# First chunk's MLP in float32 on unsplit weights, weights split later, and the scores of two units in one run, in an attention and MLP kernel

## The chip, the cores and the metric

The kernel runs on one core of one Trainium2 chip. A core has a matrix engine (TensorE, PE in the profile, with PEld for its weight loads), VectorE (DVE), ScalarE (ACT), GpSimd (POOL) and SyncE (SP, here used to issue DMAs). The metric is the device time in microseconds; less is better.

## The reference

Attention in two parts over 8 batches and 8 heads, with 512 local and 32 global rows of 64 numbers each, and then a two-layer MLP over all 8 x 544 = 4352 rows. The weights of the MLP arrive as 64-bit floats.

```python
k_all = np.concatenate([k_g, k_l], axis=2); v_all = np.concatenate([v_g, v_l], axis=2)
out_g = np.matmul(sm(scale * np.matmul(q_g, k_all.transpose(0, 1, 3, 2))), v_all)
mask = np.abs(pos[:, None] - pos[None, :]) <= 32
s_ll = np.where(mask, scale * np.matmul(q_l, k_l.transpose(0, 1, 3, 2)), -1000000000.0)
s_lg = scale * np.matmul(q_l, k_g.transpose(0, 1, 3, 2))
out_l = np.matmul(sm(np.concatenate([s_lg, s_ll], axis=-1)), np.concatenate([v_g, v_l], axis=2))
x = np.concatenate([out_g, out_l], axis=2)      # then as (4352, 512), heads side by side
h = x @ w_in                                    # 512 -> 2048
g = 0.5 * h * (1.0 + erf(h / sqrt(2)))
return g @ w_out                                # 2048 -> 512
```

## The kernel before

**Tiling.** The local rows are worked in 16 chunks of 256 rows (a batch and a half of it, `key = (b, half)`), the global rows of all batches as a seventeenth chunk `"g"`. A chunk's attention has four units `(b, half, p)`, one for each pair of heads, and gives the chunk's input x, transposed, in `xs` (512 x 256). The chunk's MLP then goes over 16 column blocks f of 128: first-layer products (`h`, four row blocks c of x, L727 to L729), gelu on ACT for two blocks at a time (`gf`), and second-layer products into two accumulators (`acc`, L758 to L760).

**Split products.** Except in the first eight units, every product is made in float32r with its operands split into a rounded part and the rest, as three passes (high x high, high x low, low x high). So each MLP product has three matmul passes, and x, the gelu output and the weights are each split by a copy (`xh`, `gh`, first half of `wi` and `wo`) and a subtraction (`xl`, `gl`, second half). The first eight units (`NF32`) multiply unsplit float32 instead.

**Weights.** Each of 32 weight tiles n (even: a block of `w_in`, odd: of `w_out`; 512 KB as 64-bit numbers) is loaded into one of seven buffers (`w_load`), turned into float32 bits in three steps (`w_1`, `w_2` on ACT, `w_3` on DVE), and split (`w_4` copies, `w_5` subtracts) into `wi` and `wo`. The first chunk's products wait for `w_5`.

**A unit's steps.** Keys and queries are loaded, transposed (for the first eight units on PE, L362 to L370, later on DVE), and copied or split; scores on PE (`st_s`, L440: pairs of matmuls on the two halves of the array's rows), masks and maxima on DVE (L459), exponentials on ACT, normalization on DVE, transposes on PE (L514 to L517), copies, and the output product (L563 in the first eight units, L550 later). `sg`, `gt`, `go` and `gx` are the global rows' scores, transposes and products.

**What sets the order.** Every step is a node with needs, buffers that it takes and frees, the engines it may run on, an assumed duration (`DUR`) and a due time. A planner in the kernel starts, on the engine that is free first, the ready step that is due first, and the instructions are issued in that order, which each engine then keeps. Due times come from a base per chunk (`C = 60.0` us each), and tables of offsets by kind (`OFF`, `OFF0`).

Of the kernel before, what the change touches and what calls it, by code (L numbers as in the profile page):

```python
# [84 lines left out]
def attn_mlp(ctx, tc, q_l, k_l, v_l, q_g, k_g, v_g, w_in, w_out, out):  # L100
# [31 lines left out]
    for half in range(2):  # L132
        m = cp.tile([P, WS + WF], BF16, name=f"mask{half}")
        nc.gpsimd.memset(m, 0.0)


        if half == 0:
            runs = [(0, 0, 128), (160, 128, 32),
                    (WS, -32, 32), (WS + 64, 0, 160)]
        else:  # L140
            runs = [(0, -32, 32), (64, 0, 128),
                    (WS, -32, 160), (WS + 192, 128, 32)]
        for c0, k0, w in runs:
# [10 lines left out]

    def copy(e, out, in_):
        if e == "a":
# [3 lines left out]
        else:  # L160
            nc.gpsimd.tensor_copy(out=out, in_=in_)

    def sub(e, **kw):
        (nc.vector if e == "v" else nc.gpsimd).tensor_sub(**kw)  # L164

# [951 lines left out]
```

## Time and profile before

| | us |
|---|---|
| median of 3 runs (lowest, highest) | 1057.42 (1057.25, 1058.53) |
| span of the profiled execution, first to last instruction | 1052.2 |
| PE without work, summed over the span | 31.1 |
| of it before 220 us | 26.0 |

The profile shows one execution. A row of its groups or of its timeline names the source line, the engine, the operation, output and inputs, the shape, and how many; in a group the two numbers after the bar are the time that its instructions cover in us and the mean of one in ns, and behind the second bar stands how long the engine was idle just before them. A timeline row has start and length in us ahead. Times of PE instructions overlap, since it works in a pipeline, so its pace is read from start to start. "PEclk" is the share of the full clock that was granted to PE.

### The profile page before, as it was taken

The page shows a single profiled execution, that of the slowest core. Times are in us where ns is not written, and L with a number is a line of the kernel's source. Part 1 is how long each engine was busy: PE and PEld are TensorE (multiplying, and loading weights), DVE is VectorE, ACT ScalarE, POOL GpSimd, SP SyncE. Part 2 cuts the span into 40 slices and gives each one's busy share as a digit, 9 for nine tenths or more (in the row PEclk, how much of TensorE's full clock was granted, in tenths as well). Part 3 has the DMA queues.
Part 4 walks back from the last instruction along what each step waited for, and adds up shares of the span by engine and source line. Part 5 has one row for each costly group of instructions (what it writes and reads, how often), then busy time and mean ns, then how long its engine had stood idle before and what let it go on. Part 6 is the DMA issues. An engine that isn't in the chain of part 4 may idle for free.

```text
span 1052.2 us, 21637 instructions
## 1 busy us (share of the span) xinstructions
PE 1021.1 (97%) x7096; PEld 911.2 (87%) x7096; DVE 716.5 (68%) x2168; ACT 745.3 (71%) x1650; POOL 355.2 (34%) x407
## 2 busy tenths in 40 slices
PE   4799999999999999999999999999999999999998
PEld 3488788889899889998998989998999989999896
DVE  5898866775867777777868777777868768661000
ACT  6886887677769686787769686787779686774231
POOL 3232345334333433234323433234323434243121
PEclk9899999999999999999999999999999999999999
DMA  8756333322222232223222332223231332101000
GB/s 243 205 149 197 84 84 64 78 51 68 45 59 38 60 74 49 56 52 79 44 63 38 65 71 47 55 53 78 44 66 38 64 67 50 46 14 34 1 21 21
DMA packets 273233, 71.27 MB, mean 68 GB/s; under 512 B 258528, under 2 KB 266720, under 8 KB 273120
## 3 DMA queue, kind: packets, MB, share of 16 engines
q1 hardware_dynamic: 269808, 65.03, 27.6%
q10 hardware_dynamic: 3312, 4.85, 1.5%
q8 instruction: 56, 0.92, 0.4%
q14 instruction: 57, 0.47, 0.1%
HBM read 60.88 MB, written 8.91 MB: 66 GB/s over the span
## 4 chain that ended last, share of the span: by engine, by line
PE 87%; DVE 3%; DMA 3%; ACT 3%; issue 2%; SPq 1%; POOL 1%; ACTq 0%; POOLq 0%; DVEq 0%
PE h L727 11%; PE h L729 11%; PE h L728 11%; PE acc L758 11%; PE acc L760 11%; PE acc L759 11%; PE o L550 5%; PE s L440 5%; PE t L514 3%; PE go L678 2%; PE sg L593 2%; DMA wraw<-in_moe_w_in_dram 1%; PE t L515 1%; ACT a_t L323 1%; PE o L563 1%
## 5 line engine op out<-in xcount | busy, mean ns | idle before, releaser
L164 POOL TENSOR_TENSOR gl<-gf,gh 128x512 fp32r<-128x512 f32 x135 | 176.7, 1309 | 459.6 <-DVE gh L159 247.4
L727 PE MATMUL h<-xh,wi 128*128 128x256 f32 x1088 | 315.0, 290 | 1.3 <-ACT xh L157 1.3
L728 PE MATMUL h<-xl,wi 128*128 128x256 f32 x1088 | 303.9, 279 | 0.5 <-POOL xl L164 0.4
L729 PE MATMUL h<-xh,wi 128*128 128x256 f32 x1088 | 303.6, 279 | 0.0
L758 PE MATMUL acc<-wo,gh 128*128 128x512 f32 x544 | 219.7, 404 | 0.0
L727 PEld LDWEIGHTS h<-xh,wi 128*128 128x128 f32 x1088 | 204.2, 188 | 12.5 <-ACT xh L157 1.7
L760 PE MATMUL acc<-wo,gh 128*128 128x512 f32 x544 | 214.9, 395 | 0.0
L759 PE MATMUL acc<-wo,gl 128*128 128x512 f32 x544 | 214.8, 395 | 0.0
L728 PEld LDWEIGHTS h<-xl,wi 128*128 128x128 f32 x1088 | 204.6, 188 | 6.8 <-POOL xl L164 0.6
L729 PEld LDWEIGHTS h<-xh,wi 128*128 128x128 f32 x1088 | 204.2, 188 | 0.0
L323 ACT ACT_TABLE_LOAD x129 | 165.5, 1283 | 40.3 <-PE h L729 38.6
L323 ACT ACTIVATE gf<-h 128x512 f32<-128x512 f32 x136 | 81.2, 597 | 76.2 <-PE h L729 73.4
L760 PEld LDWEIGHTS acc<-wo,gh 128*128 128x128 f32 x544 | 102.1, 188 | 24.5
L323 ACT ACTIVATE a_t<-a_t,sm 128x192 f32<-128x192 f32 (+1 forms) x256 | 117.0, 459 | 1.4 <-DVE sm L465 0.6
L759 PEld LDWEIGHTS acc<-wo,gl 128*128 128x128 f32 x544 | 102.4, 188 | 13.2 <-POOL gl L164 0.3
L758 PEld LDWEIGHTS acc<-wo,gh 128*128 128x128 f32 x544 | 102.2, 188 | 13.4
L164 POOL TENSOR_TENSOR vs<-vr,vs 128x512 fp32r<-128x512 f32 x56 | 72.6, 1297 | 120.1 <-ACT vs L157 53.1
L459 DVE CUSTOM_DVE_ANT_0 a_t<-s,mask 128x192 f32<-128x192 f32 (+1 forms) x256 | 80.8, 369 | 27.9 <-PE s L440 27.7
L534 DVE TENSOR_TENSOR at<-t,at 128x512 fp32r<-128x512 f32 x112 | 67.8, 619 | 23.3 <-ACT at L157 22.0
L550 PE MATMUL o<-at,vs 128*128 128x256 f32 x448 | 74.2, 288 | 0.2
L157 ACT ACTIVATE at<-t 128x512 fp32r<-128x512 f32 x112 | 59.1, 542 | 21.6 <-PE t L517 10.4
L550 PEld LDWEIGHTS o<-at,vs 128*128 128x128 f32 x448 | 63.0, 188 | 8.3 <-issue 2.1
(121 smaller groups left out, 1618.8 us busy)
## 6 DMA issues: line engine op xcount, KB each, us to landing
raws<-in_v_l_dram SPq DMA_DIRECT2D x64, 128.0 KB, 2.4
out_dram<-ob SPq DMA_DIRECT2D x32, 256.0 KB, 2.1
raws<-in_k_l_dram SPq DMA_DIRECT2D x224, 36.0 KB, 2.0
vr<-in_v_l_dram SPq DMA_DIRECT2D x116, 64.0 KB, 2.1
raws<-in_q_l_dram SPq DMA_DIRECT2D x224, 32.0 KB, 1.9
wraw<-in_moe_w_out_dram SPq DMA_DIRECT2D x12, 512.0 KB, 4.0
wraw<-in_moe_w_in_dram SPq DMA_DIRECT2D x11, 512.0 KB, 4.7
wraw<-in_moe_w_in_dram ACTq DMA_DIRECT2D x5, 512.0 KB, 4.3
```

What stands on the lines that cost most here:

```text
L157: nc.scalar.activation(out=out, in_=in_, func=AF.Copy)
L164: (nc.vector if e == "v" else nc.gpsimd).tensor_sub(**kw)
L323: nc.scalar.activation(func=func, **kw)
L459: nc.vector.tensor_tensor_reduce(out=a_t[:, j, aoff[half][i]:aoff[half][i] + w], in0=s[:, c:c + w], in1=masks[half][:, c:c + w], scale=1.0 ...
L534: nc.vector.tensor_sub(out=at[:, 1], in0=st.pop((u, "t", j))[:, :n * P].rearrange("p (n q) -> p n q", q=P), in1=at.bitcast(F32)[:, 0])
L550: nc.tensor.matmul(out=o[:, :, qsl], lhsT=l.rearrange("p s e -> p (s e)"), rhs=r, start=(n == 0), stop=(n == 3), skip_group_check=True)
L727: nc.tensor.matmul(out=h, lhsT=hi, rhs=xh, start=(c == 0 and not (key == (0, 0) and f < HQ and f % 2)), stop=False, skip_group_check=True)
L728: nc.tensor.matmul(out=h, lhsT=hi, rhs=xl, start=False, stop=False, skip_group_check=True)
L729: nc.tensor.matmul(out=h, lhsT=lo, rhs=xh, start=False, stop=(c == NCC - 1), skip_group_check=True)
L758: nc.tensor.matmul(out=acc[t], lhsT=gh[:, f % 2, tsl], rhs=hi, start=(f == 0), stop=False)
L759: nc.tensor.matmul(out=acc[t], lhsT=gl[:, f % 2, tsl], rhs=hi, start=False, stop=False)
L760: nc.tensor.matmul(out=acc[t], lhsT=gh[:, f % 2, tsl], rhs=lo, start=False, stop=(f == NF - 1))
```

## The change

The first chunk's MLP multiplies unsplit float32: x comes straight from the output product into `xf`, the weights from `w_3` (`wf`), the gelu output is not split, and each product is one float32 matmul (two instructions on PE) instead of three. Its steps wait for `w_3`, no longer for the split. `w_4` and `w_5` run later, after the last weight tile is loaded and converted and after chunk 0 has used the tile; chunk 1 waits for `w_5`. The loads of weights have 16 buffers, with at most six loads ahead of `w_1` (`NW`); half of the `w_1` steps may go to DVE. From the ninth unit on, the scores of two units are one step (`st_s2`), the second unit's in two banks of the pool of transposes. The first units' keys, queries and values have a second set of buffers (`rawb`, `vrb`), and some of these loads are issued by ACT. The global rows go to DRAM (`gu_w`) and are read back at the end (`ml_xg`). The masks are stored once for both halves. Due times and offsets are new.

```diff
-    "ah": 3.7, "al": 7.1, "b": -0.8, "c": -23.8, "e": -38.8, "g": -16.9, "gagh": 2.4, "gagl": -24.7,
...
+    "ah": (-1660.8, 999.4, -180.5, -284.0), "al": (-88.1, -183.9, -1009.5, -128.3), "b": (103.5, -531.0, -610.7, -1679.5),
...
+NW = 6
...
+    wp = ctx.enter_context(tc.tile_pool(name="wp", bufs=2 * NF + 1))
+    wr = ctx.enter_context(tc.tile_pool(name="wr", bufs=NF))
...
     def w_1(e, n):
...
+        raw = wraw[n]
+        if e == "v":
+            nc.vector.tensor_single_scalar(out=raw[:, 0::2], in_=raw[:, 0::2], scalar=29, op=ALU.logical_shift_right)
+        else:
+            nc.scalar.activation(out=raw[:, 0::2], in_=raw.bitcast(U16)[:, 1::4], func=AF.Copy, scale=2.0 ** -13, bias=-0.5 + 2.0 ** -14)
...
     def w_3(e, n):
...
+        raw = wraw.pop(n)
+        wf[n] = wp.tile([P, 512], F32, name="wf", tag="w")
+        nc.vector.scalar_tensor_tensor(out=wf[n].bitcast(I32), in0=raw[:, 1::2], scalar=3, in1=raw[:, 0::2],
                                        op0=ALU.logical_shift_left, op1=ALU.bitwise_or)
...
+    def w_4(e, i, n):
+        if i % 2 == 0:
+            wh["t"] = wr.tile([P, 1024], F32R, name="wh", tag="wr")
+        wh[n] = wh["t"][:, i % 2 * 512:i % 2 * 512 + 512]
+        copy(e, wh[n], wf[n])
 
     def w_5(e, n):
...
+        wl_[n] = lo = wp.tile([P, 512], F32R, name="wl", tag="w")
+        sub(e, out=lo, in0=wf.pop(n), in1=wh[n].bitcast(F32))
...
+    def st_s2(e, u, x):
+        st_s(e, u)
+        st_s(e, x, 1)
+
+    def st_s(e, u, other=0):
         half = u[1]
+        i = u[2] % 2
         for jj in range(2):
-            st[u, "s", jj] = ps_s.tile([P, 512], F32, name="s", tag="s")
+            st[u, "s", jj] = (ps_t if other else ps_s).tile([P, 512], F32, name="s", tag="t" if other else "s")
...
     def st_c0(e, u):
         o = st.pop((u, "o", 0))
+        x = xs[:, u[2]]
+        if u[:2] == (0, 0):
+            st["xf", u[2]] = x = xp.tile([P, CH], F32, name="xf", tag=f"xh{u[2]}")
         for j in range(2):
-            copy(e, xs[64 * j:64 * j + 64, u[2]], o[0:64, j])
+            copy(e, x[64 * j:64 * j + 64], o[0:64, j])
...
+    def gu_w(e, g, i):
+        b, p = g[0], 2 * g[1] + i
+        nc.sync.dma_start(out=xg[:, p, b * SG:b * SG + SG], in_=st.pop((g, i, "c")))
+
+    def ml_xg(e):
+        nc.sync.dma_start(out=xs, in_=xg)
...
         h = st["h", key, f // 2][:, f % 2]
+        if key == (0, 0):
+            nc.tensor.matmul(out=h, lhsT=wf[2 * f][:, c * P:c * P + P], rhs=st["xf", c], start=(c == 0 and not (f < HQ and f % 2)), stop=(c == NCC - 1), skip_group_check=True)
+            return
...
+        acc = st[key, "acc"]
+        if key == (0, 0):
+            for t in range(2):
+                nc.tensor.matmul(out=acc[t], lhsT=st[key, "gf", f // 2][:, f % 2, t * P:t * P + P], rhs=wf[2 * f + 1], start=(f == 0), stop=(f == NF - 1))
+            return
...
-    C = 60.0
+    CS = [28.0] + [106.0 + 60.0 * c for c in range(2 * B)]
+    CW = [4.3] + [3.75] * (2 * B)
...
+        step(("w4", n), w_4, (i, n), "va", due + 60.0, [("w3", wl[NF + i // 2]), ("wl", wl[-1])] + ([("w4", wl[i - 1])] if i else []), [("wr", ("h", n))] if i % 2 == 0 else [])
+        step(("w5", n), w_5, (n,), "pv", due + 61.0, [("w4", n), ("w5", wl[i - 1]) if i else ("w3", wl[-1])] + used)
...
+        elif odd:
+            step(("s", u), st_s2, (pu, u), "t", s0, [(x, y) for x in ("q1", "k1", "q2", "k2") for y in (pu, u)] + [("s", units[n - 2])],
+                 [(x, (y, "s", j)) for x, y in (("s", pu), ("t", u)) for j in range(2)] + [(x, y) for y in (pu, u) for x in ("sm", "a%d" % (y[2] % 2))],
...
+            w = [("w3", 2 * f)] if not n else [("w5", 2 * f)] if n == 1 else []
...
+        elif nm[0] == "wl" and wl.index(nm[1]) >= NW:
+            tc.add_manual_dep(ins[seen], w1s[wl[wl.index(nm[1]) - NW]], mybir.DependencyInfo(mybir.DependencyClass.Sync, mybir.DependencyReason.DATA), reason="throttle")
```

What moves is seen best in the order in which each engine gets its instructions. Three places follow; the line numbers are those of the respective kernel.

**PE, where the first MLP begins.** Before, from the output product (`o`) of the first chunk's fourth unit on; `s` are the next unit's scores, `qp` transposed queries:

```order
L563 MATMUL o_597<-ao_589,vr 64x128
L563 MATMUL o_597<-ao_593,vr 64x128
L563 MATMUL o_597<-ao_589,vr 64x128 x2
L440 MATMUL s<-kt,qt 128x192 x2
L440 MATMUL s<-kt,qt 128x224 x2
L370 MATMUL qp<-ident,raws 128x128 x2
L727 MATMUL h<-xh,wi 128x256
L728 MATMUL h<-xl,wi 128x256
L729 MATMUL h<-xh,wi 128x256
```

Now, from the output product of the first unit on (`t` are transposes of the second unit's weights):

```order
L530 MATMUL o_357<-ao_340,vr 64x128 x2
L563 MATMUL sg<-kt,gs 128x288
L705 MATMUL h<-xf,wf 128x256 x3
L480 MATMUL t<-ident,a_t_122 128x128 x2
L481 MATMUL t<-ident,ge 128x128
L483 MATMUL t<-ident,ge 128x128
L327 MATMUL qp<-ident,raws 128x128 x2
```

The first products of the MLP stand behind the first unit instead of the fourth. In all 12 of the 64 (each two instructions on PE) stand ahead of the fourth unit's output product, those of the first three head pairs with the first four weight blocks.

**PE, a run of scores in a later chunk.** Before, one unit (`k` and `q` are the split operands):

```order
L440 MATMUL s<-k_141,q_143 128x192 x2
L440 MATMUL s<-k_141,q_144 128x192 x2
L440 MATMUL s<-k_142,q_143 128x192 x2
L440 MATMUL s<-k_141,q_143 128x224 x2
L440 MATMUL s<-k_141,q_144 128x224 x2
L440 MATMUL s<-k_142,q_143 128x224 x2
```

Now, the same step for two units, between MLP products:

```order
L406 MATMUL s<-k_4792,q_4883 128x192 x2
L406 MATMUL s<-k_4792,q_4902 128x192 x2
L406 MATMUL s<-k_4797,q_4883 128x192 x2
L406 MATMUL s<-k_4792,q_4883 128x224 x2
L406 MATMUL s<-k_4792,q_4902 128x224 x2
L406 MATMUL s<-k_4797,q_4883 128x224 x2
L406 MATMUL s<-k_4931,q_5008 128x192 x2
L406 MATMUL s<-k_4931,q_5037 128x192 x2
L406 MATMUL s<-k_4956,q_5008 128x192 x2
L406 MATMUL s<-k_4931,q_5008 128x224 x2
L406 MATMUL s<-k_4931,q_5037 128x224 x2
L406 MATMUL s<-k_4956,q_5008 128x224 x2
```

The second unit's six rows follow the first one's without anything between. From the ninth unit on all 56 units go in 28 such runs.

**ACT, the head of its queue.** Before (`wraw` is a weight tile, `kt` the first unit's keys, copied from the transposes):

```order
L183 DMA wraw<-in_moe_w_in_dram 128x4x256 x2
L200 ACT_TABLE_LOAD
L200 ACTIVATE wraw<-wraw 128x512
L204 ACTIVATE wraw<-wraw 128x512
L157 ACTIVATE kt<-kp 128x320
```

Now (`vr` and `vrb` are values, `gs` the global queries):

```order
L262 DMA vr<-in_v_l_dram 32x2x64 x2
L312 DMA raws<-in_q_l_dram 128x4x64 x2
L374 ACT_TABLE_LOAD
L374 ACTIVATE gs<-qg 64x4x32 x2
L251 DMA vrb<-in_v_l_dram 128x4x64 x2
L259 DMA vrb<-in_v_l_dram 32x4x64
L259 DMA vrb<-in_v_g_dram 32x4x64
L259 DMA vrb<-in_v_l_dram 64x4x64
L262 DMA vrb<-in_v_g_dram 32x2x64 x2
L262 DMA vrb<-in_v_l_dram 32x2x64 x2
L132 ACTIVATE kt<-kp 128x320
L150 DMA wraw<-in_moe_w_in_dram 128x4x256
```

The loads of the first four units' values and of the first queries (20 issues in all, seven of them ahead of these rows) now stand ahead of the first copy, and the first weights behind it.

More of the change, by code (lines that the diff above doesn't have):

```diff
@@ L132, in attn_mlp @@
     for half in range(2):
-        m = cp.tile([P, WS + WF], BF16, name=f"mask{half}")
+        m = cp.tile([P, WF], BF16, name=f"mask{half}")
         nc.gpsimd.memset(m, 0.0)
[L137 to L143, printed above, removed]
+        for c0, k0, w in (((0, -32, 32), (64, 0, 160)) if half == 0 else ((0, -32, 160), (192, 128, 32))):
             v = m[:, c0:c0 + w]
@@ L242, in attn_mlp @@
     qraw = raws[:, 928:1184].rearrange("p (c e) -> p c e", e=32)
[L244 to L254 removed]
+    agt = lp.tile([P, 4, 2, 2, SG], F32R, name="agt")
+    agg = lp.tile([P, 2, 2, 2, SG], F32R, name="agg")
+    for i in range(2):
+        nc.vector.tensor_copy(out=agg[:, i], in_=zero)
     def quads():
@@ L665, in gu_vc @@
     def gu_vc(e, g, i):
-        copy(e, late["vgs"][:, :, 0, :], gvr)
+        if "vgs" not in st:
+            st["vgs"] = lp.tile([P, 10, 2, D], F32R, name="vgs", tag="vgs")
+        copy(e, st["vgs"][:, :, 0, :], gvr)
     def gu_vl(e, g, i):
-        t = late["vgs"]
+        t = st["vgs"]
         sub(e, out=t[:, :, 1, :], in0=gvr, in1=t.bitcast(F32)[:, :, 0, :])
     def gu_o(e, g, i):
-        a = [late["agt"][:, n] for n in range(4)] + [late["agg"][:, i]]
+        a = [agt[:, n] for n in range(4)] + [agg[:, i]]
         o = ps_s.tile([P, 2, 2, D], F32, name="go", tag="s")
@@ L735, in ml_g @@
     def ml_g(e, key, f):
[L736 removed]
+        gf = gp.tile([P, 2, CH], F32, name="gf", tag="gh") if key == (0, 0) else gp.tile([P, 2, CH], F32, name="gf", tag="gf", bufs=1)
         st[key, "gf", f] = gf
@@ L838, in attn_mlp @@
             if not odd:
-                step(("lk", u), load_kn, (u,), "s", s0 - 15.0, [], [("kn", u)], issues=5 + half, size=0.33, after=("lk", units[n - 2]) if n else None)
-                step(("lq", u), load_qn, (u,), "s", s0 - 14.0, [], [("qn", u)], issues=2, size=0.26, after=("lq", units[n - 2]) if n else None)
-            step(("tk", u), st_tkn, (u,), "t", s0 - 5.0, [("lk", pair)] + pv(("tq",)), [("h", (u, "k"))], [("kn", pair), ("kgr", b)], dur="tkn")
-            step(("tq", u), st_tqn, (u,), "t", s0 - 3.5, [("lq", pair)], [("h", (u, "q"))], [("qn", pair)], dur="tqn")
+                step(("lk", u), load_kn, (u,), "s", s0 - 15.0, [], [("kn%d" % second(u), u)], issues=5 + half, size=0.33, after=("lk", units[n - 2]) if n else None)
@@ L843, in attn_mlp @@
+                step(("lq", u), load_qn, (u,), "sa" if n < 4 else "s", s0 - 14.0, [], [("qn%d" % second(u), u)], issues=2, size=0.26, after=("lq", units[n - 2]) if n else None)
+            step(("tk", u), st_tkn, (u,), "t", s0 - 5.0, [("lk", pair)] + pv(("tq",)), [("h", (u, "k"))], [("kn%d" % second(u), pair), ("kgr", b)], dur="tkn")
+            step(("tq", u), st_tqn, (u,), "t", s0 - 3.5, [("lq", pair)], [("h", (u, "q"))], [("qn%d" % second(u), pair)], dur="tqn")
             kb, qb = [("h", (u, "k"))], [("h", (u, "q"))]
@@ L880, in attn_mlp @@
         if n < NPE and not odd:
-            step(("lv", u), load_v, (u, 2), "s", f0 - 18.0, [], [("vr0", u), ("vr1", units[n + 1])], issues=9, size=0.5, after=("lv", units[n - 2]) if n else None)
+            step(("lv", u), load_v, (u, 2), "sa" if n < 4 else "s", f0 - 18.0, [], [("vs", (u, "r"))] if second(u) else [("vr0", u), ("vr1", units[n + 1])], issues=9, size=0.5, after=("lv", units[n - 2]) if n else None)
             step(("vm", u), st_vm, (u, 2), "p", f0 - 8.0, [("lv", u)])
@@ L953, in attn_mlp @@
         for f in range(NF // 2):
             d = C0 + W * (2 * f + 2)
-            step(("g", key, f), ml_g, (key, f), "a", d, [("hc", key, x, NCC - 1) for x in (2 * f, 2 * f + 1)] if not n and 2 * f < HQ else [("h", key, 2 * f + 1) if 2 * f + 1 < NF - 1 else ("hc", key, NF - 1, NCC - 1)], [("gf", (key, f))], [("h", (key, f)) if n or 2 * f >= HQ else ("acc", "h")], table="gelu")
-            step(("gh", key, f), ml_gh, (key, f), "av", d + 0.7, [("g", key, f)], [("gh", (key, f))], early=not n)
@@ L957, in attn_mlp @@
-            step(("gl", key, f), ml_gl, (key, f), "v" if key == "g" and f == NF // 2 - 1 else "p", d + 1.3, [("gh", key, f)], [("gl", (key, f))], [("gf", (key, f))], early=not n)
+            step(("g", key, f), ml_g, (key, f), "a", d, [("hc", key, x, NCC - 1) for x in (2 * f, 2 * f + 1)] if not n and 2 * f < HQ else [("h", key, 2 * f + 1) if 2 * f + 1 < NF - 1 else ("hc", key, NF - 1, NCC - 1)], [("gf" if n else "gh", (key, f))], [("h", (key, f)) if n or 2 * f >= HQ else ("acc", "h")], table="gelu")
```

347 lines of the change are left out of this document (168 added, 179 removed), and 25 rows, old and new, of tables (DUR, OFF, OFF0).

## The prediction

> **What bounds the kernel now.** I read the page's busy times first, then sums by stage, because a mean over the whole span hides that the stages have different limits.
>
> ```profile
> PE 1021.1 (97%) x7096; PEld 911.2 (87%) x7096; DVE 716.5 (68%) x2168; ACT 745.3 (71%) x1650; POOL 355.2 (34%) x407
> ```
>
> The sums by stage (first the stretch in us and its length, then each engine's busy time and instructions):
>
> ```profile
> core 0: us, PE busy (x) PEld busy (x) DVE busy (x) ACT busy (x) POOL busy (x), PEclk, DMA share, GB/s
> 0.00:15.20 15.20, 4.89 (x18) 2.65 (x18) 4.63 (x10) 6.28 (x11) 7.72 (x28) 1.00 0.76 210
> 15.20:56.50 41.30, 31.04 (x166) 22.48 (x167) 36.61 (x107) 36.79 (x94) 9.03 (x10) 0.88 0.74 215
> 56.50:116.50 60.00, 56.73 (x376) 49.27 (x377) 50.75 (x122) 44.43 (x93) 15.74 (x18) 0.97 0.62 165
> 116.50:220.00 103.50, 101.33 (x719) 90.33 (x719) 77.74 (x242) 80.44 (x186) 45.30 (x50) 1.00 0.34 74
> 220.00:940.00 720.00, 719.91 (x5145) 650.90 (x5145) 536.00 (x1660) 543.29 (x1201) 249.65 (x279) 1.00 0.26 55
> 940.00:1052.20 112.20, 107.21 (x680) 95.59 (x678) 10.76 (x28) 34.11 (x69) 27.72 (x22) 1.00 0.06 19
> ```
>
> From 220 to 940 us TensorE (PE) is busy for 719.91 of 720 us at full clock: there only fewer or shorter PE instructions save time, and what DVE, ACT or POOL do counts only if PE comes to wait for it. The last stage has 5.0 us without PE work (its final copies and stores), which the change leaves as it is. All other idle PE time lies before 220 us: 10.3 us up to 15.2, 10.3 up to 56.5 (at a clock of 0.88), then 3.3 and 2.2. The first MLP matmul starts right at 56.5:
>
> ```profile
> 56.58 0.36 PE L727 MATMUL h<-xh,wi 128*128 128x256 f32 x1
> ```
>
> Between 15.2 and 56.5 DVE and ACT are each busy 89% of the time: they bound that stage, not PE (75%). So four terms make the sum: when the first chunk's attention is done (A), what its MLP then costs PE (B), what the joined score runs save (C), and what PE waits after that (D). All are differences against this profiled execution, whose span is 1052.2 us; the median of the runs, 1057.4, is 5.2 us more (launch and end, which the change doesn't touch), so I take the differences from the median.
>
> **A: when chunk 0's attention is done.** What DVE does in that stage:
>
> ```profile
> L208 DVE SCALAR_TENSOR_TENSOR wraw<-wraw 128x512 int32<-128x512 int32 x13 | 8.8, 687 | 0.0
> L459 DVE CUSTOM_DVE_ANT_0 a_t<-s,mask 128x224 f32<-128x224 f32 x10 | 3.8, 384 | 0.0
> L493 DVE TENSOR_TENSOR a_t<-a_t,sm 128x512 f32<-128x512 f32 x4 | 3.6, 902 | 0.1
> L459 DVE CUSTOM_DVE_ANT_0 a_t<-s,mask 128x192 f32<-128x192 f32 x10 | 3.5, 350 | 1.0 <-PE s L440 1.0
> L164 DVE TENSOR_TENSOR wo<-wraw,wo 128x512 fp32r<-128x512 f32 x4 | 2.8, 698 | 0.0
> L164 DVE TENSOR_TENSOR wi<-wraw,wi 128x512 fp32r<-128x512 f32 x4 | 2.8, 693 | 0.1
> L159 DVE CAST xh<-xs 128x256 fp32r<-128x256 f32 x3 | 1.8, 653 | 0.0
> L159 DVE CAST wi<-wraw 128x512 fp32r<-128x512 f32 x4 | 1.7, 424 | 0.1
> L159 DVE CAST wo<-wraw 128x512 fp32r<-128x512 f32 x2 | 0.8, 418 | 0.0
> L500 DVE TENSOR_TENSOR ge<-a_t,sm 128x256 f32<-128x256 f32 x2 | 0.8, 418 | 0.0
> ```
>
> In the new order DVE has, from the first mask-and-maximum step up to the copy of unit 3's output (the last input of the first MLP), no weight splits and no xh or xl: minus 8 x 0.70 (the second halves, wi and wo), 6 x 0.42 (the first halves), about 2.2 for xh and xl, and one conversion of 12 instead of 13 (0.7), also two small products that POOL takes (0.6): 11.6 us less. It has more: five first conversion steps that were ACT's (no row shows them on DVE; between 0.42, the plain copy of this size, and 0.74; I take 0.69, the step on the same tile: 3.4), a sixth unit's four mask steps (1.5) and a fifth normalization (1.3), three more 128x256 products (1.3), and small copies (0.9): 8.4. Net 3.2 us less. With the same 4.7 us of idle time DVE comes to that copy at 15.2 + 36.6 - 3.2 + 4.7 = 53.3 instead of 56.5. **A = -3.2.** With no idle time it would be 48.6 (-7.9); if the weights come late it is no earlier than now (+1). ACT's own work in that stage falls from 36.8 to about 33 by the same count, so DVE stays the later one.
>
> Nothing is won at the very start. ACT's queue now issues 20 loads ahead of its first copy, and SP eight small ones ahead of the first keys:
>
> ```profile
> 6.03 2.38 SPq L282 DMA_DIRECT2D qgr<-in_q_g_dram  x4
> 8.45 0.98 SPq L296 DMA_DIRECT2D vr<-in_v_l_dram  x2
> 13.26 1.86 PE L440 MATMUL s<-kt,qt 64*128 64x192 f32 x8
> ```
>
> At 0.5 us per issue (0.98 for two) ACT is through at about 0.7 + 10 + 1.3 for its table + 0.6, nearly 13 us; SP's keys are issued by 0.7 + 8 x 0.6 + 5 x 0.55 = 8.3. The first scores thus start behind ACT's copy, near 13.5, as now (13.26). The first weights, which head ACT's queue now, are issued at 13 to 18 us; twelve of them (6.3 MB) and 1.5 MB of attention input need 36 us at the stage's 215 GB/s, till about 50. That is just ahead of DVE, so a start no earlier than now stays in the range.
>
> **B: the first MLP in float32.** One of its products is two passes, each at half the rate, instead of three passes at the full one.
>
> ```profile
> 24.84 1.96 PE L563 MATMUL o<-ao,vr 128*64 128x128 f32 x16
> ...
> L563 PE MATMUL o<-ao,vr x16: 272/272/323, 24.8 to 26.5; 128*64 128x128 f32 x16
> ...
> 58.67 0.70 PE L593 MATMUL sg<-kt,gs 128*128 128x256 f32 x2
> ...
> 299.83 0.28 PE L728 MATMUL h<-xl,wi 128*128 128x256 f32 x1
> 299.95 0.28 PE L729 MATMUL h<-xh,wi 128*128 128x256 f32 x1
> 300.07 0.40 PE L758 MATMUL acc<-wo,gh 128*128 128x512 f32 x1
> 300.30 0.40 PE L759 MATMUL acc<-wo,gl 128*128 128x512 f32 x1
> ```
>
> (The second row gives one instruction's shortest, median and longest time in ns; "f32" stands for split operands too.) Split passes start 0.12 us apart at 256 columns and 0.23 at 512. A chunk has 192 + 96 of them: 23.0 + 22.1 = 45.1 us. A float32 pass over 128 columns takes 0.11 us: sixteen in 1.96, of which the last one's tail is 0.27, so 1.69/15; that makes 0.22 and 0.44; the two passes of 256 columns at 58.67 agree (0.70 less a start-up of 0.1 and an end of 0.16 leaves 0.22 each). 128 x 0.22 + 64 x 0.44 = 56.3, thus 11.2 us more (10.7 with 0.109 per pass, 12.5 with 0.113). But twelve of the 64 first-layer products stand in the new order ahead of unit 3's output product, where PE is idle a quarter of the time: 12 x 0.44 = 5.3 us are hidden. **B = +5.9.** Without that cover it is +11.2.
>
> The Trainium skill ("TensorE: Matmul & The Clock Gate", Weight-path perf modes — Fast Weight Load (FWL) and DoubleRow) speaks against this part: fast weight load is on for 128 weights unless the type is FP32, so a float32 product would load its stationary half more slowly. The trace's shortest float32 load is as short as a split one, in the rows under the rivals.
>
> **C: scores of two units in one run.**
>
> ```profile
> 308.56 0.28 PE L729 MATMUL h<-xh,wi 128*128 128x256 f32 x1
> 308.77 0.93 PE L440 MATMUL s<-k,q 64*128 64x192 f32 x12
> 309.63 0.39 PE L727 MATMUL h<-xh,wi 128*128 128x256 f32 x1
> 309.85 0.28 PE L728 MATMUL h<-xl,wi 128*128 128x256 f32 x1
> ...
> 309.19 0.51 PE L440 MATMUL s<-k,q 64*128 64x224 f32 x6
> ...
> L440 PE MATMUL s<-k,q x24: 268/272/355, 210.3 to 220.6; 64*128 64x192 f32 x12, 64*128 64x224 f32 x12
> ```
>
> From the last h pass to the second one behind the run are 1.29 us; without the run it would be 2 x 0.12, so a run costs 1.05. Its twelve products go as six pairs (two row halves of 64 at once), and the last three pairs, 0.51 less a tail of 0.27, are 0.12 apart. Six more pairs in the same run cost 0.72 instead of 1.05: 0.33 saved in each of 28 runs. **C = -9.3.** If only the two switches outside fall (0.09 into the run, 0.10 behind it) it is 5.3; at 0.11 per pair 10.9.
>
> A joined run needs both units' four operands and four PSUM banks at once, two of them from the pool of the transposes. Behind it on PE stand the MLP products, and for those ACT's gelu waits. In the new order the last reader of those banks (a copy and a subtraction, some 1.2 us) has about 24 MLP products, 4 us, ahead of the run; I take 0, at most 0.3 per run.
>
> **D: waits after that.** Now PE idles 3.3 + 2.2 us between 56.5 and 220, and 3% of a slower clock over 56.7 us cost 1.7: about 7. In the new kernel PE has 65 us of work from unit 3's output product to the first split product of chunk 1. In it ACT has, counted from the order, 31 conversion steps and 20 weight copies (0.56 apart, rows below), five table loads, twelve exponentials of the last three units (1.92 a unit), eight gelus and some 30 small copies:
>
> ```profile
> 28.35 0.66 ACT L200 ACTIVATE wraw<-wraw 128x512 int32<-128x512 uint16 x1
> 28.91 0.68 ACT L204 ACTIVATE wraw<-wraw 128x512 f32<-128x512 f32 x1
> L323 ACT ACT_TABLE_LOAD x129 | 165.5, 1283 | 40.3 <-PE h L729 38.6
> ```
>
> 28.6 + 6.4 + 5.8 + 4.6 + about 15 = 60 us beside 65 of PE. That is closer than now (44.4 of 60), but PE has MLP work at hand all the while, so I keep the same 7 us: **D = 0**, from -6 (no waits) to +14 (below). The splits' second halves, 20 of them on POOL at 1.3 us, run beside this and chunk 1; POOL is a third busy. The global rows' detour through DRAM costs 0: the load stands ahead of the stores of the chunk before the last, tens of us of MLP work; bare it would be some 5 us. From 220 us on ACT loses some 60 table loads, which changes nothing, as PE doesn't wait for ACT there.
>
> Sum: -3.2 + 5.9 - 9.3 + 0 = -6.6, so 1057.4 - 6.6 = **1050.8 us**.
>
> **Rivals.**
>
> (1) ACT becomes the bound of the float32 stage (slower). Place: from unit 3's output to chunk 1. Price: if PE is as idle there as in the stage from 15.2 to 56.5 (25%, with ACT at 89%), its 65 us take 87, 22 us idle instead of 7: 15 more, 1065. It decides the sign once that stage idles over 14 us. For it: 60 us of ACT work in 65, served in a fixed order. Against: in that earlier stage PE had no MLP work to fill in.
>
> (2) No earlier start: weights and keys come later, A = +1, and the joined run saves only the outer switches, C = -5.3: 1 + 5.9 - 5.3 = +1.6, 1059. That would be the change not doing what it says. That the runs stay apart is excluded by the order.
>
> (3) More is won: DVE runs without gaps (A = -7.9), C = -10.9, B = +5.4, waits after that nearly gone (D = -5): -18.4, 1039.
>
> (4) Float32 weight loads lie bare. The loads of the score product that is float32 now, and split later:
>
> ```profile
> L593 PEld LDWEIGHTS sg<-k,gs x112: 186/188/192, 121.2 to 923.9; 128*128 128x128 f32 x112
> L593 PEld LDWEIGHTS sg<-kt,gs x16: 186/240/337, 16.3 to 101.6; 128*128 128x128 f32 x16
> ```
>
> The shortest are equal (186), but the float32 ones reach 337. If each of the 192 passes paid 0.15 us more: +29, 1079. Against: a pass of 0.22 us is long enough to hide a load. By the skill's rule this would be the case; the trace's 186 speaks against it.
>
> **Chances.** Forecast, 1046 to 1055: 0.48. (3), 1038 to 1046: 0.20. (2): 0.14. (1): 0.15. (4): 0.03. What differs by less than 0.2% (2.1 us) can't be told from no change in a measurement of this kernel. Faster: 0.48 + 0.20 and a little of (2), 0.70; same: the rest of (2), 0.12; slower: (1), (4), 0.18. The range, 1041 to 1062, leaves out the far half of (3), the upper half of (1), and (4).
>
> **What would show it.** A: the first h product that needs unit 3's output starts near 53 us, twelve f32 products ahead of it. B: first-layer float32 passes 0.22 us apart, second-layer 0.44. C: score rows x24 of about 1.65 us, 28 of them. D: PE idle between there and 220 us about 7 us, and under 0.5 us from 220 to 940. Wrong if PE's waits name ACT (copies of gelu, weights) for over 14 us, or if a joined run shows idle time ahead of it.

## The result, and the profile after

| | before | changed |
|---|---|---|
| median of the runs (lowest, highest), us | 1057.97 (1057.25, 1059.07), 4 runs | 1051.65 (1050.12, 1052.00), 4 runs |
| span of the profiled execution, us | 1052.2 | 1048.3 |
| ratio of the times, 95% interval | | 0.9945 (0.9924 to 0.9967) |

The changed kernel is 6.3 us faster by the medians; 6.6 were forecast. A second set of runs gave 0.9947 (0.9930 to 0.9965), 5.4 us. So the sum was right. Its terms were not all right, and that is what the rest is about.

The busy sums by stage of the changed kernel, for the same stretches as before (stretch and length in us, then busy time and instructions of each engine, granted clock, DMA share, GB/s):

```profile
core 0: us, PE busy (x) PEld busy (x) DVE busy (x) ACT busy (x) POOL busy (x), PEclk, DMA share, GB/s
0.00:15.20 15.20, 3.25 (x10) 1.62 (x10) 2.56 (x8) 1.90 (x3) 5.57 (x22) 1.00 0.58 125
15.20:56.50 41.30, 34.98 (x211) 25.72 (x211) 32.85 (x108) 29.90 (x83) 6.31 (x8) 1.00 0.83 236
56.50:116.50 60.00, 56.48 (x265) 39.65 (x266) 48.04 (x115) 49.42 (x107) 10.41 (x15) 1.00 0.63 197
116.50:220.00 103.50, 103.50 (x734) 91.44 (x733) 76.49 (x228) 77.07 (x180) 55.74 (x53) 1.00 0.27 57
220.00:940.00 720.00, 713.95 (x5132) 651.24 (x5132) 510.54 (x1608) 486.07 (x1183) 276.59 (x310) 1.00 0.27 56
940.00:1048.30 108.30, 103.98 (x654) 93.61 (x652) 9.93 (x24) 32.57 (x65) 25.80 (x20) 1.00 0.08 24
```

Three things differ from the table of before. PE has less work up to 15.2 us (3.25 instead of 4.89): the start is later than before. From 15.2 to 56.5 it pauses 6.3 us instead of 10.3, at full clock instead of 0.88. And from 220 to 940 us, where it had hardly waited (0.09 us), it now pauses 6.05 us. What it waits for there (total us, times, longest us):

```profile
PE t L480 <- DVE agg L625: 1.6, 3, 0.7
PE t L480 <- DVE a_t L459: 1.5, 1, 1.5
PE h L709 <- ACT gf L279: 1.4, 2, 1.2
PE gx L666 <- DVE sgr L576: 0.7, 1, 0.7
```

Why the start is late stands in the timelines of ACT's and PE's instructions (start, length; in brackets the idle time ahead and what ended it; ACTq is ACT issuing DMAs):

```profile
0.74 1.06 ACTq L251 DMA_DIRECT2D vr<-in_v_l_dram  x2
...
10.20 0.93 ACTq L251 DMA_DIRECT2D vrb<-in_v_l_dram  x2
...
16.58 0.80 ACTq L262 DMA_DIRECT2D vrb<-in_v_l_dram  x2
17.43 0.44 ACT L132 ACTIVATE kt<-kp 128x320 f32<-128x320 f32 x1 [7.48 <-DMA vrb<-in_v_l_dram]
```

```profile
12.79 0.37 PE L321 MATMUL kp<-ident,raws 64*128 64x64 f32 x1
17.92 1.76 PE L406 MATMUL s<-kt,qt 64*128 64x192 f32 x8 [4.76 <-ACT kt L132]
```

The transposed keys are ready at 13.2 us (12.79 + 0.37). ACT is to copy them, but from 10.20 to 17.4 it issues nine loads, 0.8 us each on average. The first scores start at 17.92 instead of 13.26.

The float32 passes and a joined run of scores, start to start:

```profile
94.94 1.88 PE L736 MATMUL acc<-wf,gf 128*128 128x512 f32 x4
96.66 1.89 PE L705 MATMUL h<-xf,wf 128*128 128x256 f32 x8
98.38 0.27 PE L666 MATMUL gx<-ident,gos 128*128 128x128 f32 x1
...
303.21 0.39 PE L746 MATMUL acc<-wl,gh 128*128 128x512 f32 x1
303.53 1.60 PE L406 MATMUL s<-k,q 64*128 64x192 f32 x24
305.06 0.39 PE L709 MATMUL h<-xh,wh 128*128 128x256 f32 x1
305.28 0.28 PE L710 MATMUL h<-xl,wh 128*128 128x256 f32 x1
```

Four passes of 512 columns in 1.72 us are 0.43 each, eight of 256 in 1.72 are 0.215: the forecast's 0.44 and 0.22. From 303.21 to 305.28 are 2.07 us; without the run it would be 0.23 + 0.12, so the joined run costs 1.72, against 2 x 1.05 for two single ones.

### The profile page after: what moved, and what is told of

Its sections match the earlier page's. It is cut to its first block, busy times and chain, and to the rows that moved or that the text cites. A ratio compares the mean times of both kernels' runs of the same rounds, so it can differ in the third digit from the quotient of the medians.

```text
span 1048.3 us, 21420 instructions
## 1 busy us (share of the span) xinstructions
PE 1016.1 (97%) x7000; PEld 903.3 (86%) x7000; DVE 680.4 (65%) x2089; ACT 676.9 (65%) x1617; POOL 380.4 (36%) x427
## 4 chain that ended last, share of the span: by engine, by line
PE 84%; DMA 4%; ACT 4%; DVE 3%; SPq 3%; issue 1%; POOL 0%; ACTq 0%; DVEq 0%; POOLq 0%
PE h L709 11%; PE h L711 10%; PE h L710 10%; PE acc L744 10%; PE acc L745 10%; PE acc L746 10%; PE o L517 5%; PE s L406 4%; PE t L480 2%; PE acc L736 2%; PE h L705 2%; PE go L650 2%; ACT a_t L279 1%; PE sg L563 1%; DMA wraw<-in_moe_w_in_dram 1%
## 5 line engine op out<-in xcount | busy, mean ns | idle before, releaser
L709 PE MATMUL h<-xh,wh 128*128 128x256 f32 x1024 | 299.1, 292 | 1.4 <-ACT gf L279 1.4
L711 PE MATMUL h<-xh,wl 128*128 128x256 f32 x1024 | 289.7, 283 | 0.0
L710 PE MATMUL h<-xl,wh 128*128 128x256 f32 x1024 | 289.3, 283 | 0.0
L744 PE MATMUL acc<-wh,gh 128*128 128x512 f32 x512 | 206.3, 403 | 0.0
L709 PEld LDWEIGHTS h<-xh,wh 128*128 128x128 f32 x1024 | 195.0, 190 | 10.4 <-ACT gf L279 1.8
L745 PE MATMUL acc<-wh,gl 128*128 128x512 f32 x512 | 201.7, 394 | 0.0
L746 PE MATMUL acc<-wl,gh 128*128 128x512 f32 x512 | 200.6, 392 | 0.0
L710 PEld LDWEIGHTS h<-xl,wh 128*128 128x128 f32 x1024 | 195.2, 191 | 5.7 <-issue 0.7
L711 PEld LDWEIGHTS h<-xh,wl 128*128 128x128 f32 x1024 | 195.0, 190 | 0.0
L745 PEld LDWEIGHTS acc<-wh,gl 128*128 128x128 f32 x512 | 97.0, 189 | 11.3
```

What stands on the lines that cost most here:

```text
L709: nc.tensor.matmul(out=h, lhsT=hi, rhs=xh, start=(c == 0 and not (key == (0, 0) and f < HQ and f % 2)), stop=False, skip_group_check=True)
L710: nc.tensor.matmul(out=h, lhsT=hi, rhs=xl, start=False, stop=False, skip_group_check=True)
L711: nc.tensor.matmul(out=h, lhsT=lo, rhs=xh, start=False, stop=(c == NCC - 1), skip_group_check=True)
L744: nc.tensor.matmul(out=acc[t], lhsT=gh[:, f % 2, tsl], rhs=hi, start=(f == 0), stop=False)
L745: nc.tensor.matmul(out=acc[t], lhsT=gl[:, f % 2, tsl], rhs=hi, start=False, stop=False)
L746: nc.tensor.matmul(out=acc[t], lhsT=gh[:, f % 2, tsl], rhs=lo, start=False, stop=(f == NF - 1))
```

## The experiments

Each run is compared with runs of the kernel before on the same chip; "the changed kernel" stands at 0.9947, 1051.74 us (first experiment).

**1. The changed kernel once more.**

> The changed kernel once more, nothing edited: the base for the other runs. Both theories: 0.992 to 0.997 of the kernel before. Two open things are read from it. First, PE's pauses between 220 and 940 us (6 us in all in the first profile, the longest 1.5 us ahead of transposes at 311.6 us): if the order of the steps makes them, they stand at the same places with the same lengths within 0.2 us; if they are chance (DMA, clock), they move. Second, what lies around the span: 1.8 us in the changed kernel's runs; the 5.2 us that I took for the kernel before was a difference between one profiled execution and the median of other executions, and if that is all, a run of the kernel before shows the same 1.8.

Measured: 0.9947 (0.9930 to 0.9965). The pauses behind 220 us stand at the same places: 1.54 and 1.15 us near 311 us again, 0.52 at 260 (0.71 at first), 0.92 at 493 (0.65 at first). The order of the steps makes them; only the small ones vary. Around the span lie 1.7 to 2.0 us, in every run of both kernels. The 5.2 us that I took for launch and end were wrong: the profiled execution of before (1052.2) was one of its fastest; of the 67 other spans beside the experiments (1051.3 to 1059.0) two were shorter. Another thing varies: the first product that needs unit 3's output starts at 60.66 here, at 56.42 in the first profile. The later profiles with the same first loads are like this one. The first unit's output product shows where this comes from, in the first profile and here:

```profile
29.12 1.96 PE L530 MATMUL o<-ao,vr 128*64 128x128 f32 x16
```

```profile
32.55 2.79 PE L530 MATMUL o<-ao,vr 128*64 128x128 f32 x16
```

PE works more slowly at the start of both: two transposes take 0.69 us instead of 0.45, eight score products 1.76 instead of 0.97. In the first profile, as in the kernel before, its rows shorten from about 24 us on, here only from about 34. The first product of the MLP starts at 31.97 and at 36.20, so all of the 4.2 us arise there. "PEclk" reads 1.00 in both from 18 to 38 us, so it doesn't show this slower pace; what ends it isn't shown.

**2. The first key copies on DVE.**

```diff
-        x["fn"](x["on"], *x["args"])
+        x["fn"]("v" if x["name"] in (("k1", (0, 0, 0)), ("k1", (0, 0, 1))) else x["on"], *x["args"])
```

> The copies of the first two units' keys (kt) run on DVE, which is idle from 11.6 to 19.7 us, instead of on ACT behind its queue of nine loads; nothing else is moved. Theory (step A failed because ACT's issues hold the copy back): the first scores start at 13.5 to 14 us instead of 17.9, and the first h product that needs unit 3's output starts 3 to 4 us earlier, at 52 to 53.5 instead of 56.4; the time falls by 2 to 4 us. Rival 1 (weights bound the stage): scores start as early, but that product still comes at 55.5 to 56.5 because DVE or ACT then wait for weights; time within 1 us. Rival 2 (ACT's exponentials of unit 0 still stand behind the issues, near 18 us): about half, 54 to 55, 1 to 2 us less.

Measured: 0.9936 (0.9916 to 0.9955), 1.2 us less than the changed kernel, inside the interval. PE's timelines, the changed kernel of experiment 1 first, then this one:

```profile
60.66 1.99 PE L705 MATMUL h<-xf,wf 128*128 128x256 f32 x8 [1.01 <-DVE xf L134]
80.23 1.56 PE L705 MATMUL h<-xf,wf 128*128 128x256 f32 x6 [0.25 <-ACT gf L279]
```

```profile
12.84 1.82 PE L406 MATMUL s<-kt,qt 64*128 64x192 f32 x8
57.37 1.99 PE L705 MATMUL h<-xf,wf 128*128 128x256 f32 x8 [1.02 <-DVE xf L134]
80.23 1.56 PE L705 MATMUL h<-xf,wf 128*128 128x256 f32 x6 [0.70 <-ACT gf L279]
```

ACT's first step behind its loads in this run:

```profile
18.88 0.41 ACT L569 ACTIVATE sgr<-sg 64x288 f32<-64x288 f32 x1 [9.03 <-DMA vrb<-in_v_l_dram]
```

The scores start 5.4 us earlier, the first product that needs unit 3 3.3 us earlier, and at 80.23 us all of it is gone: that product starts there in both (80.27 in the first profile). It waits for a gelu, which stands on ACT behind conversions that wait for weights. That ACT's issues hold the copy back is shown; that this would shorten the time isn't. Nor did the product come at 52 to 53.5 us, as the theory has it, but at 57.37. Rival 2's cause is there: ACT's softmax work still stands behind the loads (18.88), and DVE waits 3.2 us for it. What ends the gain at 80 us is rival 1's cause, later than it had it.

**3 and 4. A product on full rows inside the joined run, or behind it.**

```diff
+    def full(u):
+        nc.tensor.matmul(out=st[u, "s", 0][:, 416:512], lhsT=st[u, "q1"][:, 0:P], rhs=st[u, "k1"][:, 0:96], start=False, stop=False, skip_group_check=True)
     def st_s2(e, u, x):
-        st_s(e, u)
+        st_s(e, u), full(u)
         st_s(e, x, 1)
```

(In the other kernel `full(x)` stands behind the last line.)

> Between the two units of each of the 28 joined score runs stands one more product that uses all 128 rows of the array (96 columns, its result is not read), so that the array is switched from half rows to full rows and back once more in each run, as when the units ran apart. Theory C (0.33 us per switch out and in, measured from single runs of before): 28 x (0.33 + 0.05 for the product) = 10.6 us more than the changed kernel. Rival (joining saves only by chance of what stands around, or the price lies in the first scores' waits): only the product itself, 28 x 0.05 = 1.4 us more.

> The same 28 extra products, but behind the second unit of each run, next to the MLP products that use full rows anyway: no switch more. Both theories: 28 x 0.05 = 1.4 us more than the changed kernel, up to 3; the difference to the run with the product in between is the price of 28 switches, 9.2 us by theory C, near 0 by the rival.

Measured: between 1.0041 (1.0027 to 1.0054), behind 0.9977 (0.9965 to 0.9989); medians 1061.32 and 1055.09, profiled spans 1060.2 and 1052.1. PE's timeline with the product between, then behind:

```profile
306.37 0.39 PE L746 MATMUL acc<-wl,gh 128*128 128x512 f32 x1
306.68 0.93 PE L406 MATMUL s<-k,q 64*128 64x192 f32 x12
307.54 0.31 PE L388 MATMUL s<-k,q 128*128 128x96 f32 x1
307.79 0.93 PE L406 MATMUL s<-k,q 64*128 64x192 f32 x12
308.64 0.38 PE L709 MATMUL h<-xh,wh 128*128 128x256 f32 x1
308.87 0.28 PE L710 MATMUL h<-xl,wh 128*128 128x256 f32 x1
```

```profile
304.76 0.39 PE L746 MATMUL acc<-wl,gh 128*128 128x512 f32 x1
305.08 1.60 PE L406 MATMUL s<-k,q 64*128 64x192 f32 x24
306.61 0.31 PE L388 MATMUL s<-k,q 128*128 128x96 f32 x1
306.76 0.35 PE L709 MATMUL h<-xh,wh 128*128 128x256 f32 x1
306.94 0.28 PE L710 MATMUL h<-xl,wh 128*128 128x256 f32 x1
```

From the pass ahead to the second one behind are 2.50 and 2.18 us (2.07 without the product). The product alone costs 0.11, not 0.05; where it splits the run, 0.32 more. 28 times 0.32 are 9.0 us (8.7 over all 28 runs, since two of them hold pauses); the medians differ by 6.2, the profiled spans by 8.1, and why it is less there stays open. Theory C holds: what is saved is the switch between half and full rows, or any break of the run by such a product, which these two kernels don't tell apart.

**5 and 6. The weights ahead of small loads on SP, without and with the copies on DVE.**

```diff
     order.sort(key=lambda e: e[:2])
+    for a, b in [(('glv', (0, 0), 0), ('wl', 11)), (('lk', (1, 0, 0)), ('wl', 18)), (('lq', (1, 0, 0)), ('wl', 18)), (('lv', (0, 1, 0)), ('wl', 18)), (('lv', (0, 1, 2)), ('wl', 24)), (('glv', (0, 0), 1), ('wl', 24))]: x = order.pop([e[2]["name"] for e in order].index(a)); order.insert([e[2]["name"] for e in order].index(b) + 1, x)
```

> On SP's queue the 25 small loads of the next chunks' values, keys and queries that stand ahead of the second batch of weights (issued from 52.6 us on), and the 15 ahead of the third (from 69.9 us on), go behind those weights. Nothing else is moved. Theory (the first MLP is paced at 80.25 us by weights that SP issues late; the start and the first chunk's attention don't count): ACT's waits for weights at 56.5 and 73.8 us (3.5 and 3.1) and DVE's at 60.2 (3.8) shrink to under 1 us, the product that starts at 80.23 to 80.27 us in all runs so far starts at 76 to 78, and the time falls by 2 to 4 us. Rival (ACT's and DVE's own work up to there, or DMA throughput, is the pace): it stays within 1 us of 80.25, and the time too.

> The same, and the first two units' key copies on DVE as in the run before with them. Theory: now the early start reaches the MLP: that product starts 3 to 6 us before 80.25, 1 to 2 us earlier than with the weights alone, and the time falls by 4 to 6 us against the changed kernel. Rival: the early start is lost again, no difference to the weights alone within 1 us.

Measured: alone 0.9940 (0.9919 to 0.9960); with the copies 0.9922 (0.9905 to 0.9938), and 0.9935 (0.9918 to 0.9951) in a second set. The same product on PE, weights alone, then both:

```profile
60.85 1.35 PE L705 MATMUL h<-xf,wf 128*128 128x256 f32 x5 [1.02 <-DVE xf L134]
...
80.01 1.67 PE L705 MATMUL h<-xf,wf 128*128 128x256 f32 x7
```

```profile
13.22 1.82 PE L406 MATMUL s<-kt,qt 64*128 64x192 f32 x8
58.08 1.99 PE L705 MATMUL h<-xf,wf 128*128 128x256 f32 x8 [1.02 <-DVE xf L134]
77.23 1.89 PE L705 MATMUL h<-xf,wf 128*128 128x256 f32 x8
```

Alone, the wait at 80 us is gone, but only 0.2 us are won: PE had come late to it (60.85) and works without a pause from there. Both together win 3.0 us there (2.0 in the profile of the second set), and the first split product of chunk 1 starts at 121.8 instead of 124.3 (122.2 in the second set). The time follows by 0.0012 to 0.0025, which the intervals don't separate from the changed kernel. So two limits stand one behind the other, the start and the weights, and each edit alone uncovers the other. Neither theory had it so: the first overrated the weights, the rival the pace of ACT and DVE.

**7. The twelve products behind unit 3.** The twelve steps of the first head pairs are put behind `("x", (0, 0, 3), 1)`, in their order, in the same way as above.

> The twelve float32 products that stand ahead of unit 3's output product go behind its copy; nothing else is moved. Step B as predicted (twelve products hidden, worth 5.3 us): 4 to 5.5 us more than the changed kernel. Rival (the product at 80.25 us waits for weights whatever comes before, so most of that cover is worth nothing): PE fills its pauses between 56 and 80 us (1.9 to 3.7 us) instead, and the time rises by 0 to 2.5 us.

Measured: 0.9978 (0.9964 to 0.9992), 0.0031 or 3.3 us above the changed kernel; in the profiles the first split product of chunk 1 starts 4.85 us later (129.15 instead of 124.30). Between the two theories, nearer to the cover as predicted (5.3).

**8. Half of the first chunk's MLP.**

```diff
-            nc.tensor.matmul(out=h, lhsT=wf[2 * f][:, c * P:c * P + P], rhs=st["xf", c], start=(c == 0 and not (f < HQ and f % 2)), stop=(c == NCC - 1), skip_group_check=True)
+            if f < HQ or c < 2: nc.tensor.matmul(out=h, lhsT=wf[2 * f][:, c * P:c * P + P], rhs=st["xf", c], start=(c == 0 and not (f < HQ and f % 2)), stop=(c == (NCC - 1 if f < HQ else 1)), skip_group_check=True)
...
-            for t in range(2):
+            for t in range(2 if f % 2 == 0 else 0):
```

> Leaves out, in the first chunk's MLP, half of the first-layer products from the fifth weight block on (24 of 64) and half of the second-layer ones (16 of 32): 24 x 0.43 + 16 x 0.86 = 24 us less work for PE, of which about 18 behind 80.25 us; all loads, conversions and splits stay. Forecast D (PE bounds the float32 stage behind 80 us, ACT and the weights have room): the first split product of chunk 1, at 124.3 us so far, starts 15 to 18 us earlier, and the time falls as much. Rival 1 (ACT, with 60 us of work, is right behind PE): it starts at most 8 us earlier, and PE's pauses name ACT or the weights for the rest.

Measured: 0.9946 (0.9924 to 0.9969): by the median nothing is won by 24 us less work for PE. But the eight executions fall in two groups: six of 1052.0 to 1054.3 us, at a mean clock of 0.988 to 0.990, and two of 1046.4 and 1046.6, at 0.993 and 0.995, some 5 us below the changed kernel. The profiled one (1054.2 us) is of the first group. In it the first split product of chunk 1 starts at 123.99. Busy sums by stage, and what PE waits for up to there (the changed kernel of experiment 1 has 23.37 of 24 us of DVE, and 24.00 of PE, in the last stretch):

```profile
60.00:80.00 20.00, 14.56 (x71) 10.63 (x72) 16.51 (x44) 17.27 (x37) 2.27 (x5) 0.88 0.81 263
80.00:100.00 20.00, 18.08 (x92) 13.40 (x91) 14.54 (x37) 15.98 (x39) 2.69 (x4) 0.87 0.72 245
100.00:124.00 24.00, 17.84 (x79) 10.29 (x78) 23.62 (x56) 20.58 (x43) 11.22 (x11) 0.93 0.27 51
```

```profile
PE t L480 <- DVE xs L134: 4.4, 1, 4.4
PE gx L666 <- DVE gos L661: 3.0, 1, 3.0
PE sg L563 <- DVE sm L425: 2.5, 2, 1.9
PE s L406 <- DVE q L139: 2.0, 1, 2.0
```

DVE is busy for nearly all of the last 24 us, and every wait names it. So rival 1's mechanism was right behind PE, with DVE in ACT's place. The lower granted clock takes a part too: 0.88, 0.87 and 0.93 of these three stretches are 6.7 us lost, beside 13.5 us of waits. So the float32 stage is nearly balanced: more work for PE costs (experiment 7), and 24 us less gain nothing in most executions and some 5 us in the two at the higher clock, of which there is no profile.

**9. Filling the pauses of the kernel before.**

```diff
         x["fn"](x["on"], *x["args"])
+        for n in range({("o", (0, 0, 0), 1): 2, ("sg", (0, 0, 2)): 6, ("sg", (0, 0, 3)): 1, ("s", (0, 1, 0)): 3}.get(x["name"], 0)):
+            fl = fl if n else ps_o.tile([P, DM], F32, name="fill", tag="acc1")
+            for m in range(2): nc.tensor.matmul(out=fl[:, 0:P], lhsT=ident, rhs=ident, start=True, stop=True, skip_group_check=True)
```

> The kernel before, with twelve products of 0.44 us put on PE (identity by identity, the result is not read) at four places between 28 and 49 us where it waits for copies: 5.3 us of work in 6.4 us of pauses, about as much as the twelve float32 products of the change put there. Theory (part of the gain is the granted clock, which is 0.89 and 0.77 in the kernel before at 30 to 60 us, where PE pauses, and 1.00 in the changed kernel): the clock there rises to 1.00, its mean from 0.994 to 0.996 to 0.998, and the time falls by 1.5 to 4 us although PE has more to do. Rival (the clock falls for another reason, or costs nothing there, as PE waits anyway): no gain, 0 to 2 us more.

Measured: 0.9996 (0.9981 to 1.0012). The clock from 30 to 45 us rose to 1.00, but stayed at 0.77 from 45 to 60, and fell to 0.91 from 110 to 150, behind a pause of 3.2 us. The mean clock of the executions was 0.992 to 0.998, beside 0.991 to 0.998 without the products. The profiled execution was the slowest of the twelve (1060.0 us, clock 0.992); eleven of the twelve were at 0.995 or more, beside nine of 17 without the products. 5.3 us more work cost nothing, but the gain that the theory asked for isn't there: inconclusive.

**10. A second-layer product ahead of three pauses.** On top of experiment 6, `("mo", (c, 0), 15)` goes ahead of `("t", (c + 1, 0, 0), 1)` for c = 3, 5 and 6.

> The kernel with the weights ahead and the first key copies on DVE once more, as the base of the next run: 0.9905 to 0.9938 of the kernel before, about 1049.2 us.

> The same, and at three of the pauses behind 220 us (0.67 to 0.92 us each, near 491, 727 and 843 us, where transposes wait for a DVE subtraction) the last second-layer product of the chunk goes ahead of the transposes. Theory (the pauses come from the order alone; PE has ready work a few steps later): the three pauses vanish, 2.2 us less than the run beside it, nothing new late. Rival (the DVE subtraction that waits is late for all that follows): the pause reappears one or two steps on, and less than 0.7 us are won.

Measured: 0.9926 (0.9911 to 0.9941), beside 0.9935 (0.9918 to 0.9951) without: 0.7 us less by the medians, inside the intervals. The pauses at 491, 725 and 842 us are gone, and nothing new is late (PE's pauses from 220 to 930 us: 4.8 us instead of 6.5). Less than the 2.2 us expected were seen in the time. The reason in the profiled execution is the clock behind the longest pause, which is still there. Busy sums of this kernel around it:

```profile
309.00:313.40 4.40, 1.71 (x13) 1.16 (x11) 4.16 (x13) 4.34 (x15) 0.00 (x0) 0.92 0.36 59
313.40:319.00 5.60, 5.60 (x26) 5.60 (x27) 3.39 (x10) 5.51 (x9) 1.27 (x1) 0.50 0.23 36
```

The pause is followed by 5.6 us at half the clock, in which PE works without a pause and does 26 instructions. In experiment 1 the 5.6 us behind the same pause (315.4 to 321.0) ran at 1.00.

**11. Filling the longest pause.** On top of experiment 10, three of the products of experiment 9 behind `("h", (2, 0), 3)` and two behind `("t", (2, 1, 0), 1)`.

> The kernel with three pauses removed, and in its longest pauses (1.54 and 1.15 us around 311 us, where PE waits for exponentials and a gelu) stand five products of 0.44 us whose result is not read. Theory (a pause of PE of 2 to 3 us is followed, in some executions, by some 5 us at half the clock, which costs 2.5 us and makes the spread between runs): no slow stretch behind 313 us, a mean clock of 0.997 or more in nearly all runs, and a median 0 to 1.5 us lower than without the products. Rival (the clock falls for reasons that pauses don't set): clock and spread as before, 0 to 0.5 us more.

Measured: 0.9911 (0.9889 to 0.9932), median 1047.06 (1046.36 to 1047.94), clock 0.997 to 1.000 in its four runs. The stretch of above in this kernel:

```profile
313.40:319.00 5.60, 5.33 (x40) 4.90 (x39) 4.15 (x12) 5.51 (x9) 1.30 (x1) 1.00 0.32 52
```

PE does 40 instructions in it. There is no slow stretch in the profiled execution, as the theory has it; but without the products it is absent from some profiles too (experiments 1 to 4), so one execution doesn't show that they removed it, and the interval overlaps with that of experiment 10, so the gain itself isn't shown. This kernel has the lowest ratio of all; against the changed kernel its interval (0.9889 to 0.9932) and that of experiment 1 (0.9930 to 0.9965) only touch.

## Why the prediction was right, step by step

**A was wrong (-3.2 forecast; -0.2 and +4.1 in two profiles).** Two steps failed. The first is "ACT is through at nearly 13 us". I took 0.5 us for each of its issues. The first eleven took 0.66 each, the nine behind them 0.8, with pauses between them, so that ACT came to the key copy at 17.43. The second is "with the same 4.7 us of idle time". DVE's work was counted well: from the first mask step to the first product that needs unit 3's output it is busy for 32.9 and 33.2 us in the two profiles, and for 33.2 in experiment 2 (36.6 - 3.2 = 33.4 forecast). But it idles for 3.8, 7.5 and 9.6 us there. In experiment 2 the first step is mended (scores at 12.84), and the product still comes at 57.37 instead of 53.3: DVE waits for ACT, behind the loads (3.2 us), for PE, which works at the slower pace of the start up to about 30 us there (3.3), and for weights (1.7). And A was no term by itself: experiments 2, 5 and 6 show that what the start wins is lost again at 80 us, unless the weights come sooner too.

**B was right (+5.9 forecast).** 128 x 0.215 + 64 x 0.43 = 55.0 us instead of 56.3, +9.9 for +11.2 (at 0.113 per pass it would have been +12.7, not +12.5); the cover was worth 3.3 to 4.9 instead of 5.3. So +5 to +7. By the fast weight load rule (the Trainium skill, "TensorE: Matmul & The Clock Gate", Weight-path perf modes — Fast Weight Load (FWL) and DoubleRow) each pass would have paid for a slower load of weights; passes 0.215 apart show none. What I didn't see is that the price isn't marginal: in the profile of experiment 8, with 24 us less for PE, chunk 1's first split product starts only 0.3 us sooner, since DVE stands right behind and the clock is lower.

**C was right (-9.3 forecast; 28 x 0.33 is 9.2).** From 115 us on, 56 single runs at 1.05 us cost 58.8. Of the 28 joined ones 26 cost 1.72 each; the two near 276 and 387 us hold pauses, 1.0 us in all (0.3 at most was allowed for one run). Together they cost 49.1: -9.7. Experiments 3 and 4 show the mechanism.

**D was wrong (0 forecast; about +2.4 by the first profile).** The pauses from 56.5 to 220 us fell from 5.4 to 3.5 us, and the clock from 56.5 to 116.5 rose from 0.97 to 1.00 (1.7 us). In return PE pauses 6.05 us from 220 to 940, where I forecast under 0.5, and where the kernel before has 0.09. By the timelines, ACT's eight exponentials of two units stand together now, and transposes and a gelu wait behind them (1.5 and 1.2 us near 311 us); and other transposes need a bank that a DVE subtraction, behind waiting key transposes, frees late. I had counted that the second unit's banks would be free in time for the scores, which held in all but two of the 28 runs, and not what the joined steps do to ACT and DVE.

**Why the sum held.** With the first profile's A the terms are -0.2, +5.0 (9.9 less 4.85), -9.7 and +2.4, -2.5 in all, and its span is 3.9 us below that of before: some 1.4 us stay open. In the second profile A is 4.2 us worse, but chunk 1's first split product starts at 124.30 in it and at 124.35 in the first, and its span is only 0.6 us longer: those 4 us don't reach the end, so +4.1 doesn't belong in a sum. The output products behind the first eight units, 448 of which take 53.2 us start to start instead of 57.8, are nearly all C again: 39 of them stood beside a single run of scores and took 0.21 or 0.22 us there instead of 0.12, 3.9 us in all. By the medians the gain is 5.4 to 6.3 us, 1.5 to 2.4 more than by the first two profiled executions. The executions of before spread widely, and the clock goes with it: of the 23 beside experiment 5, the nine at 0.991 have spans of 1056.0 to 1058.5 us, the others 1052.3 to 1055.9. In all, the mean clock was 0.990 to 0.998 for before, 0.996 to 1.000 for the changed kernel. Why the old order draws the lower clock more often isn't settled: experiment 9 gave no gain. So that the sum was right is in part luck: A and D came out 3.0 and 2.4 us worse than forecast, B and C 0.9 and 0.4 better, and the rest was made up by some 1.4 us that stay open and by 1.5 to 2.4 us between executions, for which no term stood.

## What to carry to other kernels

- When an engine issues loads and computes, count its issues at the rate that the trace shows for a long run of them (0.66 to 0.8 us here), and look which copy stands behind them; a load that moves to an idle engine's queue isn't free.
- A term that brings one stage forward counts only if the next limit is later: look for the point that does not move when the start does (80.23 us here), and try the edits in pairs.
- Where two engines are both nearly full in a stage, taking work from one can gain little (at most some 5 of 24 us here), while adding to it costs most of its price (3.3 to 4.9 of 5.3 us); test both directions before giving such a change a price.
- When a sum comes out right, compare its terms one by one: here two were off by 2.4 and 3.0 us, the same way, and effects outside the sum hid it.
